# Pooled attention and a max-out MoE on one core: leftover queries of both heads in two column tiles, two pairs in query parts, constant matmuls ahead of the first K

## The chip, the cores and the metric

The kernel runs on one core of a Trainium2 chip. Its time is in device microseconds (us) for one execution of the whole program, the median of several. Beside it stands the profile of one execution, whose span runs from the first instruction to the end of the last.

Engines by their names in the profile: PE is TensorE, the matrix engine (PEld are its weight loads), ACT is ScalarE, DVE is VectorE, POOL is GpSimd, SP is SyncE, which here only issues DMAs. A matmul of TensorE holds one operand as weights in its 128x128 array and streams the other through it. An array can be used whole (128*128 in the profile), as two halves of 64 rows each (64*128), or as two halves of 64 columns each.

## The reference

```python
q, k, v: (8, 8, 1152, 64)             # batch, heads, sequence, head width
q_pool = q.reshape(B, H, S // 2, 2, D).mean(axis=3)          # 576 queries a head
scores = (1 / sqrt(D)) * q_pool @ k^T
attn = exp(scores - max) / sum
x = (attn @ v).transpose(0, 2, 1, 3).reshape(B * 576, 512)   # 4608 tokens of width 512
h1, h2 = x @ w1, x @ w2                                      # 512 -> 1024
out = max(h1, h2) @ w_out                                    # 1024 -> 512, float32
```

Inputs and the output are float32; the kernel multiplies in bfloat16 and sums in float32.

## The kernel before, in words

**Work.** The 64 heads are 32 pairs, two heads of one batch each; a pair's heads share the array as two row halves, 64 rows of head width each. For each pair K and Q are loaded, cast (Q's neighbouring rows are added: that is the pooling), and transposed, by TensorE for the first pairs and by transposing DMAs later. Scores come out transposed, keys on the partitions: per pair nine key tiles of 128 by 576 queries. All pairs' score columns are put end to end and cut into 324 groups of 512 columns (`W`); one group fills a bank for each head, and one ScalarE exp of 128x1024 writes it to `et` in SBUF as bfloat16. `et` has room for two pairs, and the columns of a pair are overwritten by the pair after the next.

**AV.** When a pair's last group is out, `av_jobs` (L471) queues two jobs, one a head. A job is five units, chunks of 128 queries each; a unit is nine matmuls, with 128 columns of `et` as weights and 65 columns of V (64 and a column of ones, which gives the sum of the exps) streaming. 576 queries are four chunks and a half: the fifth covers 64 queries that are wanted and 64 that aren't (columns of the next key tile, or of a pad behind the last). `norm` then takes the reciprocals of the sums and multiplies, on VectorE, into `xnat`, which is transposed into `xT` (by DMA, or by TensorE for the first and the last batch and the last pair of each).

**MoE.** max(h1, h2) @ w_out is computed as relu(x @ (w1 - w2)) @ w_out + x @ (w2 @ w_out). `w21_jobs` makes w2 @ w_out once; `h_jobs` make the relu part for runs of tokens once `xT` holds all four pairs of them; `p_job` makes 128 tokens of the output with twelve matmuls. From some group on (`NARROW`) these run as `Pair`: two jobs share the array as two row halves (L407), in the shape of the scores, so that TensorE needn't change shape between the two.

**Order.** Nothing is scheduled on the chip: while the program is built, `Plan` keeps an estimate of each engine's time, and the loop at L1095 picks TensorE's next unit from what would be ready: a group of scores, an AV unit, MoE units, transposes. `cover` is the estimate of how much exp work ScalarE still has ahead. An AV job once begun goes on whenever anything else or nothing is up (`begun`, L1111); it begins when `cover` is above `START` (1.2 us). All instructions are then emitted in that order, with semaphores where one waits for another.

**Start.** The first pair's K comes in two parts (`K_CUT`, 4 and 5 tiles), cast by ScalarE (`cast_k0`), its queries in two (`Q_CUT`, 256 and 320), added by VectorE. The first pair's score columns are laid out in these two query parts (`strips`, L510), all others in one.

```python
def strips(i):
    for q0, q1 in ((0, Q_CUT), (Q_CUT, SQ)) if i == 0 else ((0, SQ),):
        for t in range(NT):
            yield t, q0, q1
```

The functions that the change touches, with their line numbers:

## Time and profile before

| | |
|---|---|
| median of 3 runs | 372.58 us (371.25 to 373.16) |
| the profiled execution | 372.56 us |
| its span | 370.8 us |
| TensorE, matmuls | 356.4 us busy, 5,918 |
| ScalarE | 315.1 us busy, 305.4 of them exps (336) |
| VectorE | 139.3 us busy |
| GpSimd | 163.1 us busy |
| HBM | 62.91 MB read, 9.44 MB written |

How to read it: a line of a group gives line, engine, operation, output and inputs, their shapes and how often; then the group's busy time in us, the mean of one in ns, the engine's idle time just before them and what ended it. A line in order of time gives its start in us, how long it and those merged with it took together, the engine, and how many. Matmuls overlap on TensorE, so the mean of one (some 190 ns even for a short one) is the time from its start to its end, not the pace at which they follow each other; the pace is read from a stretch of many.

### The profile page before, as it was taken

What the parts mean: (1) busy time and instruction counts of PE and PEld (TensorE: products, weight loads), DVE (VectorE), ACT (ScalarE), POOL (GpSimd) and SP (SyncE); (2) the same over time, 40 slices, a digit from 0 to 9 for tenths busy, and PEclk for the clock granted to TensorE, in tenths of its full rate; (3) what the DMA queues carried; (4) which work ended last, traced back from release to release, by engine and by line L of the source; (5) the groups of instructions that cost most, each with busy time, mean ns of one, the idle gap of its engine ahead of it and who ended that gap; (6) DMA issues with size and microseconds to landing.
All of it is one profiled execution on the core that took longest, in us unless ns stands there. A gap on an engine that the chain in (4) does not pass through costs nothing.

```text
span 370.8 us, 13126 instructions
## 1 busy us (share of the span) xinstructions
PE 356.4 (96%) x5918; PEld 226.2 (61%) x5918; DVE 139.3 (38%) x310; ACT 315.1 (85%) x352; POOL 163.1 (44%) x135
## 2 busy tenths in 40 slices
PE   3799999999899999999999999999999999999996
PEld 2466656656565666666647666766865657665544
DVE  3266864522342244323422332534232424345211
ACT  4999999999899999998898998999999898982211
POOL 2855596464525725482384555545545501000000
PEclk9999999999999999999999999999999999999999
DMA  8999999999999999999999999999999982020145
GB/s 282 408 389 402 359 217 247 220 288 249 344 196 262 282 283 236 280 261 167 359 239 256 269 251 275 299 252 281 331 289 272 272 133 60 2 59 2 23 92 113
DMA packets 91128, 88.10 MB, mean 238 GB/s; under 512 B 63424, under 2 KB 64192, under 8 KB 91072
## 3 DMA queue, kind: packets, MB, share of 16 engines
q1 hardware_dynamic: 90640, 86.87, 92.1%
q8 instruction: 46, 0.75, 0.9%
q10 hardware_dynamic: 432, 0.39, 0.4%
q14 instruction: 10, 0.08, 0.1%
HBM read 62.91 MB, written 9.44 MB: 195 GB/s over the span
## 4 chain that ended last, share of the span: by engine, by line
PE 82%; ACT 12%; DMA 4%; DVE 1%; issue 0%
PE sps L550 18%; PE fb L401 17%; PE fb L407 16%; PE sps L407 15%; PE sps L401 15%; ACT et L557 12%; DMA xT<-xnat 3%; DMA qraw<-in_q_dram 1%; DVE stage L766 0%; PE fb L455 0%; DVE kT L462 0%; DVE qp L378 0%; PE fb L427 0%; PE fb L625 0%; DVE xnat L490 0%
## 5 line engine op out<-in xcount | busy, mean ns | idle before, releaser
L557 ACT ACTIVATE et<-sps 128x1024 bf16<-128x1024 f32 (+1 forms) x336 | 305.4, 1016 | 21.1 <-PE sps L550 19.0
L550 PE MATMUL sps<-qpT,kT 64*128 64x256 bf16 (+7 forms) x1162 | 121.3, 287 | 3.9 <-ACT et L557 2.9
L370 POOL TENSOR_TENSOR qp<-qraw 64x576 bf16<-64x576 f32 x62 | 88.7, 1431 | 62.0 <-DMA qraw<-in_q_dram 38.0
L550 PEld LDWEIGHTS sps<-qpT,kT 64*128 64x128 bf16 x1162 | 47.5, 95 | 53.3 <-ACT et L557 27.7
L384 POOL TENSOR_SCALAR vE<-vraw 128x1152 bf16<-128x1152 f32 x32 | 37.7, 1179 | 57.7 <-DMA vraw<-in_v_dram 36.0
L401 PEld LDWEIGHTS fb<-vE,et 128*128 128x128 bf16 x1755 | 55.7, 97 | 11.1 <-issue 5.7
L401 PE MATMUL fb<-vE,et 128*128 128x65 bf16 x1755 | 61.2, 193 | 0.0
L346 POOL TENSOR_SCALAR kbf<-kraw 128x1152 bf16<-128x1152 f32 x31 | 36.1, 1165 | 29.6 <-DMA kraw<-in_k_dram 26.3
L401 PEld LDWEIGHTS sps<-vE,et 128*128 128x128 bf16 x1125 | 35.7, 97 | 7.3 <-issue 3.3
L401 PE MATMUL sps<-vE,et 128*128 128x65 bf16 x1125 | 39.4, 193 | 0.0
L407 PE MATMUL sps<-xT,wd 64*128 64x512 bf16 (+6 forms) x384 | 36.4, 296 | 0.5 <-DMA xT<-xnat 0.3
L407 PE MATMUL fb<-xT,wd 64*128 64x192 bf16 (+5 forms) x352 | 35.1, 306 | 1.4 <-DMA xT<-xnat 1.4
L407 PE MATMUL fb<-wo,stage 64*128 64x512 bf16 x256 | 36.3, 376 | 0.0
L736 DVE TENSOR_SCALAR stage<-fb 128x512 bf16<-128x512 f32 (+4 forms) x38 | 20.9, 588 | 25.9 <-PE fb L407 24.0
L736 DVE TENSOR_SCALAR stage<-sps 128x512 bf16<-128x512 f32 (+3 forms) x38 | 22.6, 629 | 20.7 <-PE sps L407 17.6
L488 DVE RECIPROCAL rc<-fb 128x5 f32<-128x5 f32 x39 | 7.6, 195 | 58.2 <-PE fb L401 58.2
L407 PE MATMUL sps<-wo,stage 64*128 64x512 bf16 x192 | 27.8, 376 | 0.0
L766 DVE COPY stage<-fb 128x512 f32<-128x512 f32 x16 | 10.3, 687 | 37.3 <-PE fb L407 37.3
L407 PEld LDWEIGHTS fb<-xT,wd 64*128 64x128 bf16 x352 | 16.4, 94 | 9.7 <-DMA xT<-xnat 1.9
L407 PEld LDWEIGHTS sps<-xT,wd 64*128 64x128 bf16 x384 | 16.5, 94 | 9.3 <-DMA xT<-xnat 0.5
L766 DVE COPY stage<-sps 128x512 f32<-128x512 f32 (+1 forms) x16 | 10.2, 671 | 31.2 <-PE sps L401 17.4
L490 DVE TENSOR_TENSOR xnat<-fb,rc 128x320 bf16<-128x320 f32 x39 | 19.2, 491 | 1.3
(65 smaller groups left out, 217.6 us busy)
## 6 DMA issues: line engine op xcount, KB each, us to landing
vraw<-in_v_dram SPq DMA_DIRECT2D x32, 576.0 KB, 6.7
kraw<-in_k_dram SPq DMA_DIRECT2D x31, 576.0 KB, 6.2
qraw<-in_q_dram SPq DMA_DIRECT2D x31, 576.0 KB, 6.0
out_dram<-stage SPq DMA_DIRECT2D x70, 128.0 KB, 4.1
xT<-in_moe_w_dram SPq DMA_DIRECT2D x4, 512.0 KB, 11.8
stage<-in_moe_w_out_dram SPq DMA_DIRECT2D x4, 512.0 KB, 15.2
stage<-in_moe_w_dram SPq DMA_DIRECT2D x4, 512.0 KB, 13.1
kT<-kbf SPq DMA_TRANSPOSE x27, 5.7
```

Source lines behind the costliest of these rows:

```text
L346: op("POOL", lambda g: g.tensor_scalar(kbf[s][:, :, :, :].rearrange("p t h d -> p h t d"), kraw[r][:, :, :, :], 1.0, 1.0, ALU.mult, ALU.mu ...
L370: op("POOL", lambda g, half=half, a=a: g.tensor_tensor(qp[s][:, :, half, :], a[:, :, 0, :], a[:, :, 1, :], ALU.add), r=[f"qraw{r}"], w=[f" ...
L384: op("POOL", lambda g: g.tensor_scalar(vE[r][:, :, :, 0:D].rearrange("p t h d -> p h t d"), vraw[r][:, :, :, :], 1.0, 1.0, ALU.mult, ALU.m ...
L401: last = e.matmul(fb[ms[0]][:, at:at + rhs.shape[-1]], lhs, rhs, start=start, stop=stop)
L407: last = e.matmul(fb[m][:, at:at + rhs.shape[-1]], lhs[rows(half)], rhs[rows(half)], start=first, stop=fin)
L488: dve(lambda e: e.reciprocal(rc[half][:, :], a[:, :, 64:65]), [f"f{m}"], [f"rc{half}"], 0.19)
L490: dve(lambda e: e.tensor_tensor(xnat[xs][:, i % NHP, :, half * D:half * D + D], a[:, :, 0:D], rc[half][:, :].unsqueeze(2).to_broadcast([P, ...
L550: last = e.matmul(sps[r][:, h, col:col + hi - lo], kT[i % 3][rows(h), t, :], qpT[i % 3][rows(h), lo:hi], start=True, stop=True)
L557: op("ACT", lambda e: e.activation(et2[:, :, c:c + z - a], sps[r][:, :, a - g * W:z - g * W], EXP, scale=scale), r=[f"s{r}"], w=keys + [f" ...
L736: dve(lambda e: e.tensor_scalar_max(to, a, 0.0), [f"f{m}"], w, 0.1 + many * size / 960.0)
L766: dve(lambda e: e.tensor_copy(osb[o][:, 0:n], fb[m][:, 0:n]), [f"f{m}"], [f"osb{o}", f"f{m}"], 0.1 + n / 966.0)
```

## The change

1. **Leftover queries.** A job of AV now has units for whole chunks only (four). The leftover 64 queries of both heads are one unit of the second head's job (`ends`): 18 matmuls with 64 weight columns each, the heads alternating. Head 0 writes partitions 0 to 63, head 1 partitions 64 to 127 of the second head's bank: two column tiles. It has a shape of its own in the plan ("c"). `norm` takes the reciprocal of four columns for the first head and five for the second, multiplies four chunks for each, and the leftover of each head in a multiplication of its own on 64 partitions. The pad of 64 columns in `et` goes; the unused half of `xnat`'s last chunk is set to zero once.
2. **Query parts.** Pairs 2 and 3 (`halves`) are laid out as pair 2's first 256 queries, pair 3's first 256, pair 2's other 320, pair 3's other 320. Each part has AV jobs, a normalization and a transpose of its own. What must be read before a place of `et` is overwritten is now kept by the place (`needs_av`, keys of 64 columns) and no longer by the pair.
3. **Start.** A memset of ones and nine matmuls of 128x512 on it (`warm_up`), whose results nothing reads, stand ahead of the first query transposes. The first K comes by DMA in 2 and 7 tiles, is cast in 2, 2 and 5, and transposed in the same cuts. The order of the first loads changes (the first weights come after three more loads).
4. **Choice of the next unit.** The fixed thresholds become rows of digits, one for every 5 us of the plan's time. An AV job once begun may pause (`hold`). Where nothing is up for more than 0.12 us, the plan waits in steps of 0.05 us and chooses again. The plan's estimates for instruction fetch and for transposing DMAs change, which alters no instruction but the order.

```diff
+ORDER = dict(
+    first="k2 v1 q2 k3 k4 q3 w0 q4 v2 w2 v3 w1",
+    halves=(2, 3),
+    k_cuts=(0, 2, 4, 9),
+    q_cut=256,
+    warm=9,
...
+    start="0056465136572767164476550756344413564146064671544542152344732214530673110601",
+    pause="3046380040400300000000800390900003030040704300700009039000040003000064000848",
...
-                self.pages[k] = t + 1.65 + 0.9 * max(0.0, self.dma_free - t)
+                self.pages[k] = t + (5.7 if self.dma_free > t + 0.5 else 3.0)
...
-            seen = self.dma_free + (1.2 if mode == "t" else 0.8)
+            seen = self.dma_free + (2.2 if mode == "t" else 0.8)
...
-        et = sbuf([P, 4 * PW + HP], BF16, "et")
+        et = sbuf([P, 4 * PW], BF16, "et")
...
             def ones(g):
-                g.memset(et[:, 4 * PW:], 0.0)
+                for s in range(2):
+                    g.memset(xnat[s][:, :, NCH, :], 0.0)
...
+        def warm_up():
+            op("DVE", lambda e: e.memset(kbf[1][:, 0, :, :], 1.0), w=["kbf1"], cost=0.1)
+            for n in range(WARM):
+                op("PE", lambda e: e.matmul(
+                    fb[0][:, :].rearrange("p (a x) -> p a x", x=P), kbf[1][:, 0, :, :].rearrange("p h d -> p (h d)"),
+                    kbf[1][:, 0:1, :, :].rearrange("p t h d -> p t (h d)").to_broadcast([P, 4, P]),
+                    start=True, stop=True), r=["kbf1"], w=["f0"], cost=0.427, n=2)
...
+            def ends(e, m):
+                at = (NCH - j0) * 66
+                for t in range(NT):
+                    for half in range(2):
+                        a = half * 2 * PW + spot(i, t, NCH * P)
+                        last = e.matmul(fb[m][rows(half), at:at + 65], et[:, a:a + HP], vE[vs][:, t, half, 0:65],
+                                        start=t == 0, stop=t == NT - 1)
+                return last
+
             def norm(half):
+                jf = min(j1, NCH)
+                both = half and j1 > NCH
...
                 def evac(m):
...
+                    for h in range(2 if both else 0):
+                        dve(lambda e, h=h: e.tensor_tensor(
+                            xnat[xs][0:HP, i % NHP, NCH, h * D:h * D + D], a[rows(h), n, 0:D],
+                            rc[half][rows(h), n:n + 1].to_broadcast([HP, D]), ALU.mult),
...
-            return [Job("a", [mm_unit(reads(half, sb), 0.264, chunk(half, sb)) for sb in range(NCH + 1)],
-                        norm(half), nb=i) for half in range(2)]
+            jobs = []
+            for half in range(2):
+                units = [mm_unit(reads(sb, P), 0.264, chunk(half, sb)) for sb in range(j0, min(j1, NCH))]
+                if half and j1 > NCH:
+                    units.append(Unit(reads(NCH, HP), 0.29, "c", go=ends, many=18))
+                jobs.append(Job("a", units, norm(half), nb=(i, part)))
+            return jobs
...
+        def order():
+            for i in range(NPAIR):
+                if i in HALVES:
+                    if i == HALVES[0]:
+                        for part in range(2):
+                            for p in HALVES:
+                                yield p, part, *spans(p)[part], p if part else HALVES[0]
...
-        load_k(0, 0, K_CUT, "ACT")
-        load_k(0, K_CUT, NT)
+        load_k(0, 0, K_CUTS[1], "ACT")
+        load_k(0, K_CUTS[1], NT)
         load_q0(q_half, QU, "qraw0", "d_q0")
-        cast_k0(0, K_CUT, "kraw0.0")
+        warm_up()
+        for lo, hi in zip(K_CUTS, K_CUTS[1:]):
+            cast_k0(lo, hi, "kraw0" if lo else "kraw0.0")
         cast_q0(0, q_half, "qraw0.0", "a")
-        cast_k0(K_CUT, NT, "kraw0")
...
-            begun = [c for c in avs if len(running[c[3]].job.units) <= NCH]
-            if begun and (rest or not up):
+            begun = [c for c in avs if len(running[c[3]].job.units) < running[c[3]].job.full]
+            level, pause, chain = 0.8 + 0.1 * knob("start"), knob("pause"), knob("chain")
+            hold = pause and begun and (up and cover < 0.1 * pause if plan.mode != "s"
+                                        else cover <= level and (rest or up))
+            if chain < 9 and plan.mode != "s":
+                level = 0.2 * chain
+            if begun and not hold and (rest or not up):
                 emit_unit(running[min(begun)[3]])
...
+                soonest = min(first_up[0], 1e9 if ts is None else ts)
+                if now() + 0.12 < soonest < 1e9:
+                    plan.free["PE"] = now() + 0.05
```

More of the change, by code (lines that the diff above doesn't have):

```diff
@@ L296, in bass_funnel_attn__then__act_maxout2_kernel, with knob @@
         plan = Plan()
+        FIRST, HALVES, Q_CUT = ORDER["first"], ORDER["halves"], ORDER["q_cut"]
+        K_CUTS, WARM, DEPTH = ORDER["k_cuts"], ORDER["warm"], ORDER["depth"]
+        K_PE, Q_PE, X_PE = range(ORDER["k_pe"]), ORDER["q_pe"], ORDER["x_pe"]
+        NAR, CALM, AHEAD, GATE = ORDER["narrow"], ORDER["calm"], ORDER["ahead"], ORDER["gate"]
+        def knob(name):
+            row = ORDER[name]
+            return int(row[min(len(row) - 1, int(now() / ORDER["bin"]))])
         op = plan.op
@@ L469, in ktrans_pe, with av_jobs @@
             return jobs
-        def av_jobs(i):
+        def av_jobs(i, part):
             b, h0 = i // NHP, 2 * (i % NHP)
-            es = i % 2
             vs = i % 3
             xs = b % 2
-            need = [f"et{es}.{g - first(i)}" for g in range(first(i), after(i))] + [f"vE{vs}", "pad"]
+            j0, j1 = (x // P if x < SQ else NCH + 1 for x in spans(i)[part])
             def chunk(half, sb):
@@ new lines, in norm, with xn_of @@
+                return evac
+            jobs = []
[5 more added lines that the diff above has]
+            return jobs
+        def xn_of(i, part=None):
+            return [f"xn{i // NHP % 2}.{2 * (i % NHP) + half}.{p}" for half in range(2)
+                    for p in ((0, 1) if part is None or i not in HALVES else (part,))]
@@ L963, in refill @@
             kinds = [r.job.kind for r in running]
-            for kind in "qkxa" + ("wh" if queue["a"] and "p" in kinds else "wph"):
-                while queue[kind] and spare and bank_at(spare[0]) <= now() + (9.0 if tail else 0.3):
+            for kind in "qkxa" + ("wh" if queue["a"] and "p" in kinds else "whp" if knob("weights") else "wph"):
+                while queue[kind] and spare and bank_at(spare[0]) <= now() + (9.0 if tail else 0.1 * knob("look")):
                     wide = queue[kind][0].two or NARROW <= nxt < NGR and queue[kind][0].split
-                    if wide and (len(spare) < 2 or pairs >= (1 if queue["a"] else 2)):
+                    if wide and (len(spare) < 2 or pairs >= (1 if queue["a"] and knob("lanes") else 2)):
                         break
@@ L1008, in emit_scores @@
             scores(g)
-            for p in pairs_of(g):
-                if g == after(p) - 1:
-                    queue["a"].extend(av_jobs(p))
+            for part in sorted(part for part, last in ends_in.items() if last == g):
+                queue["a"].extend(av_jobs(*part))
             nxt += 1
```

256 lines of the change are left out of this document (144 added, 112 removed).

## The prediction

> **What bounds the kernel now.** I read the busy shares first, then the slices, then the chain of waits, then the busy time by stage and the order of time at both ends.
>
> ```profile
> span 370.8 us, 13126 instructions
> PE 356.4 (96%) x5918; PEld 226.2 (61%) x5918; DVE 139.3 (38%) x310; ACT 315.1 (85%) x352; POOL 163.1 (44%) x135
> ...
> PE   3799999999899999999999999999999999999996
> ...
> ACT  4999999999899999998898998999999898982211
> ...
> PE 82%; ACT 12%; DMA 4%; DVE 1%; issue 0%
> ```
>
> TensorE is busy for 96% of the span and carries 82% of the chain that ended last. ScalarE is at 85%, but its slices fall to 2 and 1 in the last four, where TensorE stays at 9 but for the very end. So there are two stages: exps and everything else side by side until about 332 us, then a tail that TensorE works through alone. The end is set by TensorE's backlog: what doesn't fit beside the exps is paid for in the tail.
>
> By stage (columns: window, its sum, then busy time of PE, PEld, DVE, ACT, POOL):
>
> ```profile
> 10.00:20.00 10.00, 7.87 (x128) 4.99 (x128) 2.48 (x7) 10.00 (x12) 7.60 (x6) 1.00 1.03 405
> 20.00:40.00 20.00, 18.87 (x356) 12.84 (x351) 12.68 (x28) 19.97 (x24) 11.37 (x9) 1.00 1.04 397
> 40.00:80.00 40.00, 40.00 (x626) 23.33 (x625) 20.98 (x38) 38.72 (x44) 25.14 (x18) 1.00 1.09 260
> 80.00:120.00 40.00, 38.58 (x667) 23.98 (x663) 13.74 (x31) 36.10 (x40) 19.94 (x17) 1.00 1.12 258
> ...
> 280.00:320.00 40.00, 39.68 (x749) 26.13 (x745) 14.53 (x36) 37.23 (x43) 11.34 (x9) 1.00 0.73 163
> ...
> 340.00:350.00 10.00, 10.00 (x76) 5.04 (x74) 3.19 (x5) 3.17 (x6) 0.00 (x0) 1.00 0.01 2
> 350.00:360.00 10.00, 10.00 (x48) 4.50 (x47) 1.38 (x2) 0.81 (x3) 0.00 (x0) 1.00 0.44 95
> ```
>
> TensorE idles for 2.1 us in 10 to 20, 1.1 in 20 to 40 and 1.4 in 80 to 120, and hardly otherwise. In the first of these ScalarE is busy for all 10 us: there the exps bound. From 40 us on TensorE is full while ScalarE has 1.3 to 3.9 us to spare per 40. So time taken from TensorE's work after some 40 us comes off the end nearly one for one, whether it is used to fit more MoE matmuls beside the exps or to feed ScalarE sooner.
>
> **The change part by part.**
>
> The span is 370.8 us and this execution's time 372.56 us, so 1.76 us lie around the span; the median of the three runs, 372.58, is the same within 0.02, and I sum against 372.56.
>
> *1. Leftover queries.* Before, every pair's AV is five chunks of nine 128x65 matmuls for each head; the fifth covers 64 real queries and 64 that aren't wanted. That is 18 of 90 matmuls a pair, 576 of 2,880. After, these 576 have 64-column weights, the heads alternating between the lower and the upper half of the array's columns. The rows that price them:
>
> ```profile
> 18.05 1.53 PE L401 MATMUL fb<-vE,et 128*128 128x65 bf16 x45
> ...
> 20.40 0.45 PE L401 MATMUL fb<-vE,et 128*128 128x65 bf16 x9
> ...
> 20.78 0.39 PE L550 MATMUL sps<-qpT,kT 64*128 64x448 bf16 x4
> ...
> 21.11 0.45 PE L401 MATMUL fb<-vE,et 128*128 128x65 bf16 x9
> ```
>
> 45 matmuls end 1.53 us after the first begins. One alone has a mean of 193 ns:
>
> ```profile
> L401 PE MATMUL fb<-vE,et 128*128 128x65 bf16 x1755 | 61.2, 193 | 0.0
> L401 PEld LDWEIGHTS fb<-vE,et 128*128 128x128 bf16 x1755 | 55.7, 97 | 11.1 <-issue 5.7
> L550 PE MATMUL sps<-qpT,kT 64*128 64x448 bf16 x140 | 25.0, 351 | 0.0
> L550 PE MATMUL sps<-qpT,kT 64*128 64x64 bf16 x144 | 14.2, 191 | 0.6 <-ACT et L557 0.6
> ```
>
> (1530 - 193) / 44 = 30 ns from start to start, weight load included, though one load has a mean of 97 ns: the loads are hidden behind other matmuls. Removed: 576 x 30 = 17.3 us. No row shows two column tiles. The nearest that shows two halves of the array at work at once is this one, with row halves:
>
> ```profile
> 337.96 0.20 PE L625 MATMUL sps<-ident,xnat 64*128 64x64 bf16 x1
> 337.96 0.20 PE L625 MATMUL fb<-ident,xnat 64*128 64x64 bf16 x1
> ...
> 338.00 0.19 PE L625 MATMUL sps<-ident,xnat 64*128 64x64 bf16 x1
> ...
> 338.03 0.19 PE L625 MATMUL sps<-ident,xnat 64*128 64x64 bf16 x1
> ...
> 338.09 0.19 PE L625 MATMUL sps<-ident,xnat 64*128 64x64 bf16 x1
> ```
>
> The two halves start in the same hundredth, and the next pair 30 to 40 ns later; from 337.96 to 338.09 are four steps, 33 ns each. The upper bound is no overlap: 576 x 30 = 17.3 us, no saving, and worse if the loads come into the open (a rival below). The lower bound is a pair in the time of one matmul: 288 x 30 = 8.6 us. I take the row pairs' 33 ns, 288 x 33 = 9.5 us, because they are the same kind of case: two small tiles, alternating. Saved: 17.3 - 9.5 = 7.8 us.
>
> The Trainium skill speaks against this: TensorEngine Tiling (Array Packing), section Restrictions and Gotchas, says that column tiling excludes fast weight load. TensorE: Matmul & The Clock Gate, section LDWEIGHTS, then gives one column per 1/1.2 ns, as an estimate 53 ns for 64 columns; with 18 such loads in a row a pair's leftover would be 0.96 us instead of 0.54, and the sum would come to some 387 us. No run so far shows a load of 64 columns.
>
> *2. Changes of tile shape.* In the rows at 20.40 to 21.11, nine AV matmuls need 9 x 30 = 0.27 us, yet the scores behind them start after 0.38: 0.11 for the change from whole array to row halves. Those scores are 448 and 64 columns wide; 448 cost 351 - 191 = 160 ns more than 64 in the mean of one, or 0.4 ns a column, so 512 need about 0.21, and AV starts after 0.33: 0.12 for the way back. In the built programs' instruction order TensorE changes shape 181 times before and 200 times after: the leftover is a shape of its own, but there are fewer whole-array stretches. 19 x 0.11 = +2.1 us. That no change costs extra where it falls into a wait would make it 0; full price is the upper bound. I take +2.1, since TensorE hardly waits.
>
> *3. The start.*
>
> ```profile
> 4.59 0.63 ACT L352 ACTIVATE kbf<-kraw 128x512 bf16<-128x512 f32 x1 [2.01 <-DMA kraw<-in_k_dram]
> ...
> 4.88 0.39 PE L427 MATMUL fb<-ident,qp 64*128 64x64 bf16 x4 [4.88 <-DVE qp L378]
> ...
> 5.28 0.61 PE L455 MATMUL fb<-ident,kbf 128*128 128x128 bf16 x4
> ...
> 5.49 0.74 ACT L352 ACTIVATE kbf<-kraw 128x640 bf16<-128x640 f32 x1 [0.26 <-DMA kraw<-in_k_dram]
> ...
> 6.40 1.03 PE L550 MATMUL sps<-qpT,kT 64*128 64x256 bf16 x8 [0.52 <-DVE kT L462]
> ...
> 7.05 1.94 ACT L557 ACTIVATE et<-sps 128x1024 bf16<-128x1024 f32 x2 [0.83 <-PE sps L550]
> ...
> 8.34 1.15 POOL L346 TENSOR_SCALAR kbf<-kraw 128x1152 bf16<-128x1152 f32 x1 [6.71 <-DMA kraw<-in_k_dram]
> ...
> 9.32 15.69 ACT L557 ACTIVATE et<-sps 128x1024 bf16<-128x1024 f32 x17 [0.33 <-PE sps L550]
> ...
> 10.07 1.14 PE L455 MATMUL fb<-ident,kbf 128*128 128x128 bf16 x9
> ...
> 15.40 0.68 PE L455 MATMUL fb<-ident,kbf 128*128 128x128 bf16 x9
> ```
>
> The same nine K transposes take 1.14 us at 10.07 and 0.68 at 15.40: TensorE starts at half pace, although the granted clock reads 1.00. The nine constant matmuls of 512 columns put work ahead of the first K. At half pace (0.8 ns a column) they take up to 3.7 us and, begun near 1 us, end near 5, when the first query transposes were due anyway (4.88); bounds: those are 0.3 us late, or nothing is. K comes in cuts of 2, 2 and 5 tiles. The two ScalarE casts of before, 0.63 for 4 tiles and 0.74 for 5, give 0.11 a tile and 0.19 fixed, so the last two casts, 0.41 and 0.74, follow the second part of K (landed by 5.49) until about 6.65, and the first exp can start there instead of at 7.05. The third exp, at 9.32 now, would follow two (1.94) at about 8.6; but the second group's scores now stand behind seven K transposes, so I take 8.8. ScalarE bounds this stage, so the whole program shifts: -0.5 us, bounds -1.0 and +0.3.
>
> *4. Pairs 2 and 3 in query parts.* 18 more score pairs (1,198 matmuls for 1,162) over the same columns, nine query transposes, one more normalization each. At 30 ns or less an instruction that is under 1 us, in a stage where TensorE has 1.1 us idle: 0, bounds 0 and +1. Their first 256 queries reach the MoE sooner, but in the instruction order as many MoE columns stand ahead of the 64th score group as before (26,600 before, 25,900 after, half-array ones counted half), so no gain is booked.
>
> *5. Normalization.* Per pair the two heads' reciprocal and multiplication were 195 + 491 ns each. Now four chunks each, and two narrow multiplications:
>
> ```profile
> L490 DVE TENSOR_TENSOR xnat<-fb,rc 128x320 bf16<-128x320 f32 x39 | 19.2, 491 | 1.3
> L488 DVE RECIPROCAL rc<-fb 128x5 f32<-128x5 f32 x39 | 7.6, 195 | 58.2 <-PE fb L401 58.2
> L639 DVE COPY xT<-fb 128x64 bf16<-128x64 bf16 x6 | 1.1, 182 | 0.0
> ```
>
> Four fifths of the streaming plus twice about 182 ns (the nearest 64-wide row) add about 0.2 us a pair, 6 us in all, hidden behind VectorE's 62% idle time. What it delays is the release of the second head's bank, by some 0.3 us; if nothing else were ready, that would cost 32 x 0.3 = 9.6 us. MoE units and the other bank are there to run: 0.
>
> *6. Pauses and time-dependent thresholds* decide only order. In that order the work up to the last score group is 1 us longer for the shape changes and otherwise equal (columns weighed at 0.4 ns), and the work behind it falls from 34.8 to 27.8 us: 7 us less tail, which agrees with 1 to 3. Which waits appear, order doesn't tell.
>
> ```profile
> L407 PE MATMUL fb<-xT,wd 64*128 64x512 bf16 x96 | 13.6, 377 | 1.4 <-DMA xT<-xnat 1.4
> ```
>
> Bounds: the 1.4 us that MoE waited for a transposing DMA goes, with most of the 3.2 us before 40, together -4; or new waits of like size appear, +3. I take 0. The removed memset of a pad and those added on 64-wide rows lie on POOL, idle until 8.34; the reordered first loads cost SP nothing new in number, and the weights still arrive before their first use in the order.
>
> Sum: -7.8 + 2.1 - 0.5 = -6.2, so 372.56 - 6.2 = **366.4 us**.
>
> **The rivals.**
>
> *Loads in the open (slower).* At the leftover of every pair, 64-column weights aren't loaded beside the matmul that runs. If a load is half of the 97 ns of a 128-column one, 48 ns, and the 18 queue up, the leftover takes 0.87 us for 0.54 before: 32 x 0.33 = +10.6; with +2.1 - 0.5 that is 384.8 us. It decides against the change from 27 ns a matmul on: 576 x (30 - 27) = 1.7 covers points 2 and 3. For it: no row shows such loads hidden. Against it: whole-array loads of 97 ns are hidden at a pace of 30, and so are those for row halves. The skill's rule above is this rival.
>
> *No overlap, loads hidden.* The tiles take turns at 30 ns: saving 0, time 372.56 + 2.1 - 0.5 = 374.2, no change to be told. For it: the tiles share all rows, which the row halves don't. Against it: they share no columns and no weights.
>
> *The order gains too.* Shape and overlap as forecast, and the waits fall by the 4 us of point 6: 362.4. For it: there are such waits, 1.4 and 2.1 + 1.1 us. Against it: early idle time is ScalarE's bound, not an order's.
>
> **How the numbers follow.** Forecast 0.66, order gains 0.13, no overlap 0.09, loads in the open 0.12. The forecast's own range: the pair at 30 to 40 ns, the start and half the waits' bounds give 363.5 to 369.5. Leaving out 384.8, and the outer halves of the others, the range is 361 to 372. About 0.5% (1.9 us, near the spread of the three runs) can't be told from no change. Faster: 0.66 + 0.13 + 0.02 = 0.81; same: 0.07; slower: 0.12.
>
> **What would show it.** Right: a leftover group of 18 lasting about 0.3 us plus the last one's 0.19; the last score group near 331, and the tail from there to TensorE's end shorter by 6 to 7 us; the third exp near 8.8; the nine transposes at 10 us in 0.7; VectorE up by 6 us. Wrong: a group of 18 over 0.6 us between starts; the last score group late by more than 3 us; waits of TensorE on VectorE's narrow multiplications; the idle time of TensorE between 40 and 330 grown.

## The result, and the profile after

| kernel | median, us | lowest to highest | runs |
|---|---|---|---|
| before | 372.67 | 371.08 to 376.04 | 20 |
| changed | 369.49 | 365.77 to 374.54 | 20 |

The changed kernel takes 0.9887 of the time of before, with a 95% interval of 0.9861 to 0.9913: 1.1% faster, where the forecast of 366.4 us meant 1.65%. This ratio leaves out executions in a slower state, among them six of the changed kernel's 20 (371.48 us and up); with all of them in, the medians above give 0.9915. The median lies inside the forecast's range.

Two executions of the changed kernel were profiled: one of 373.06 us, in which TensorE's clock was halved twice, and one of 367.81 us. Where not said otherwise, "changed" below is the second; its span is 366.1 us, 4.7 less than the 370.8 of before. First its page: busy time by engine, slices, and the chain that ended last.

```profile
span 366.1 us, 13557 instructions
PE 354.9 (97%) x6093; PEld 226.8 (62%) x6096; DVE 151.5 (41%) x394; ACT 313.8 (86%) x350; POOL 164.3 (45%) x136
...
PE   8789999998999999999999999999999999999996
...
ACT  5999999997999999999999998999979998895311
...
PE 89%; DMA 5%; ACT 2%; POOL 1%; DVE 1%; issue 1%; SPq 0%; POOLq 0%
```

TensorE still ends everything, and at 97% of a shorter span. VectorE has 151.5 us for 139.3 before. The first digit of TensorE's slices, 8 for 3, is the nine constants. By stage, with the columns of before (window, length, then busy time of PE, PEld, DVE, ACT, POOL):

```profile
10.00:20.00 10.00, 8.81 (x135) 5.71 (x136) 3.17 (x9) 9.30 (x12) 9.67 (x8) 1.00 1.04 405
20.00:40.00 20.00, 18.13 (x391) 13.29 (x388) 15.35 (x37) 19.82 (x24) 10.24 (x8) 1.00 1.04 399
40.00:80.00 40.00, 39.52 (x721) 25.93 (x718) 21.95 (x55) 38.72 (x44) 27.35 (x19) 1.00 1.12 281
80.00:120.00 40.00, 38.80 (x670) 24.68 (x668) 14.62 (x39) 36.59 (x41) 21.12 (x17) 1.00 1.10 264
```

From 10 to 40 us ScalarE was busy for 29.12 us, where it was busy for 29.97 before: the start got worse, not better. From 40 to 120 TensorE is idle for 1.7 us, about as before (1.4), but not for the same reason, as will be seen. The end, on TensorE, in order of time: the last score group, and the last matmuls, of the changed kernel and then of before.

```profile
333.35 0.40 PE L654 MATMUL sps<-qpT,kT 64*128 64x512 bf16 x2
...
361.92 1.04 PE L458 MATMUL sps<-wo,stage 128*128 128x256 bf16 x8
```

```profile
330.99 0.38 PE L550 MATMUL sps<-qpT,kT 64*128 64x512 bf16 x2
...
366.69 1.04 PE L401 MATMUL sps<-wo,stage 128*128 128x256 bf16 x8
```

The last score group starts at 333.4 (331.0 before), and TensorE ends at 363.0 (367.7): 29.6 us of tail for 36.7. The tail got 7.1 us shorter, as forecast, and reached its start 2.4 us late. The question is where those 2.4 us, and some more in the median, went.

### The profile page after: what moved, and what is told of

Same layout as the page of the kernel before. It is cut to its first block, busy times and chain, and to the rows that moved or that the text cites. A ratio compares the mean times of both kernels' runs of the same rounds, so it can differ in the third digit from the quotient of the medians.

```text
span 371.3 us, 13557 instructions
## 1 busy us (share of the span) xinstructions
PE 357.2 (96%) x6093; PEld 228.3 (61%) x6096; DVE 151.0 (41%) x394; ACT 314.2 (85%) x350; POOL 164.9 (44%) x136
## 4 chain that ended last, share of the span: by engine, by line
PE 89%; ACT 5%; DMA 2%; issue 1%; POOL 1%; SPq 1%; DVE 0%; POOLq 0%
PE fb L464 20%; PE sps L654 20%; PE sps L464 19%; PE sps L458 13%; PE fb L458 13%; ACT et L661 5%; PE fb L549 3%; DMA vraw<-in_v_dram 2%; PE sps L549 1%; PE sps L730 0%; DVE stage L840 0%; POOL qp L427 0%; POOL vE L441 0%; PE fb L512 0%; POOL kbf L403 0%
## 5 line engine op out<-in xcount | busy, mean ns | idle before, releaser
L654 PEld LDWEIGHTS sps<-qpT,kT 64*128 64x128 bf16 x1198 | 49.8, 95 | 47.5 <-ACT et L661 21.8
L464 PE MATMUL sps<-xT,wd 64*128 64x256 bf16 (+5 forms) x424 | 62.4, 295 | 1.2 <-issue 1.2
L464 PE MATMUL fb<-xT,wd 64*128 64x256 bf16 (+6 forms) x408 | 60.5, 297 | 2.7 <-issue 2.5
L464 PE MATMUL fb<-wo,stage 64*128 64x512 bf16 x272 | 59.0, 376 | 0.0
L464 PE MATMUL sps<-wo,stage 64*128 64x512 bf16 x208 | 49.4, 376 | 0.0
L458 PEld LDWEIGHTS fb<-vE,et 128*128 128x128 bf16 x1296 | 42.8, 98 | 10.0 <-issue 5.6
L840 DVE TENSOR_SCALAR stage<-sps 128x512 bf16<-128x512 f32 (+4 forms) x43 | 25.4, 607 | 37.5 <-PE sps L464 34.5
L464 PEld LDWEIGHTS sps<-xT,wd 64*128 64x128 bf16 x424 | 30.0, 94 | 10.4 <-issue 1.5
L464 PE MATMUL fb<-w,xT 64*128 64x512 bf16 x136 | 30.4, 377 | 0.0
L840 DVE TENSOR_SCALAR stage<-fb 128x512 bf16<-128x512 f32 (+3 forms) x36 | 21.5, 610 | 13.5 <-PE fb L464 12.5
L464 PE MATMUL sps<-w,xT 64*128 64x512 bf16 x104 | 26.5, 377 | 0.0
```

The source lines that it names most:

```text
L458: last = e.matmul(fb[ms[0]][:, at:at + rhs.shape[-1]], lhs, rhs, start=start, stop=stop)
L464: last = e.matmul(fb[m][:, at:at + rhs.shape[-1]], lhs[rows(half)], rhs[rows(half)], start=first, stop=fin)
L654: last = e.matmul(sps[r][:, h, col:col + hi - lo], kT[i % 3][rows(h), t, :], qpT[i % 3][rows(h), lo:hi], start=True, stop=True)
L840: dve(lambda e: e.tensor_scalar_max(to, a, 0.0), [f"f{m}"], w, 0.1 + many * size / 960.0)
```

## The experiments

Each run was timed against the kernel before on the same chip; ratios are to it, with a 95% interval. Rows that the changed kernel and an experiment have in common bear different line numbers where the experiment's edit moved them.

**The changed kernel again** gave the profile above.

> The changed kernel unchanged, for a second profile. In the first profile TensorE loses 2.5, 1.5 and 1.2 us at three places to the arrival of its own instructions, and its clock is halved from 10.75 to 20.99 us and from 273.6 to 277.0. Theory A (what is missing from the forecast is lost to late instructions and the clock, which vary from run to run): these places or their lengths differ here, and the time differs with them. Rival (a fixed cost of the new order, the same in each run): the same losses at the same places. Time 366 to 371 us.

370.56 us in 6 runs, ratio 0.9899 [0.9849, 0.9949]. The gain is there, and the spread is too: one kernel, 367.81 to 371.76.

**Are the two column tiles at work at once?** The one edit makes the tiles take turns: all nine multiplications of one head, then all nine of the other.

```diff
-                for t in range(NT):
-                    for half in range(2):
+                for half in range(2):
+                    for t in range(NT):
```

> The leftover's 18 matmuls in the same 64-column shape, but head 0's nine first and then head 1's nine, so that neighbours use the same half of the columns; order otherwise kept. If the two column tiles work side by side, and the gain is theirs: a group takes 18 x 30 = 0.54 us instead of 0.31, 32 x 0.23 = +7.4 us, some 376. If a load of 64 columns is exposed when neighbours share a tile: 0.87 us a group, +18 us. Rival (the pace of the leftover doesn't count because other work bounds): within 2 us of the changed kernel.

374.47 us in 12 runs, ratio 1.0029 [0.9989, 1.0069]: the whole gain is gone. The same leftover in the two orders of time, changed kernel first (start, length from the first start to the last end, count):

```profile
58.48 1.27 PE L458 MATMUL fb<-vE,et 128*128 128x65 bf16 x36
59.68 0.47 PE L549 MATMUL fb<-vE,et 128*64 128x65 bf16 x18
60.09 0.61 PE L654 MATMUL sps<-qpT,kT 64*128 64x64 bf16 x8
```

```profile
59.70 1.27 PE L458 MATMUL fb<-vE,et 128*128 128x65 bf16 x36
60.89 0.66 PE L549 MATMUL fb<-vE,et 128*64 128x65 bf16 x18
61.48 0.61 PE L654 MATMUL sps<-qpT,kT 64*128 64x64 bf16 x8
```

One such matmul has a duration of 0.195 us, so from these rows the 18 starts lie within 0.47 - 0.195 = 0.275 us when the heads alternate, and within 0.465 when they take turns. The starts in the traces give 0.28 for 31 of the 32 pairs (0.51 for one) and 0.46 for all 32: 33 ns for two, or 27 ns for each. The tiles do work at once. 32 pairs times 0.18 make 5.8 us. How much of it reaches the median is less sure: the two profiled executions differ by 5.8 (373.61 and 367.81), but 0.9 of that was lost before the fortieth exp had ended (45.47 and 44.54), and on that chip the medians differ by 3.9 us and the ratios by 0.013, or 4.8 us. The loads, in the groups by line and form (busy time, mean ns):

```profile
L549 PEld LDWEIGHTS fb<-vE,et 128*64 128x64 bf16 x468 | 9.5, 111 | 1.8 <-issue 0.4
L549 PE MATMUL fb<-vE,et 128*64 128x65 bf16 x468 | 12.5, 197 | 0.0
```

A load of 64 columns takes 111 ns, more than one of 128 columns took for the whole array (97). It isn't sped up, as the section Restrictions and Gotchas of TensorEngine Tiling (Array Packing) in the Trainium skill has it; but at 16 to 27 ns from start to start it is hidden all the same, so the rule doesn't set the time.

**Does the start matter, and the constants?** Two kernels: one with the nine constants at 16 columns in place of 512, and one which has that and also moves the transposes of the second pair's first keys behind the next score group.

```diff
-                    fb[0][:, :].rearrange("p (a x) -> p a x", x=P), kbf[1][:, 0, :, :].rearrange("p h d -> p (h d)"),
-                    kbf[1][:, 0:1, :, :].rearrange("p t h d -> p t (h d)").to_broadcast([P, 4, P]),
+                    fb[0][:, 0:16], kbf[1][:, 0, :, :].rearrange("p h d -> p (h d)"),
+                    kbf[1][:, 0, 0, 0:16],
```

> The nine constant matmuls stream 16 columns instead of 512; the order of all instructions is kept. If the warm-up gains what was forecast (third exp earlier by 0.5 us): slower than the changed kernel by 0.5 us or a little more. Rival: TensorE's clock falls back to half at 10.75 us because too little follows, and the warm-up only moves the slow stretch to a worse place: then the clock opens near 13 us as before the change, and the time falls by 1 to 2 us.

> The constant matmuls with 16 columns, and the first half of the second pair's K transposes, with its copy, behind the score group that follows it instead of ahead. If the start lost time because TensorE stood at these transposes (until GpSimd's cast, 9.8 us) with scores ready behind them: the gap of ScalarE at 10.6 to 11.1 us closes and the 20th exp ends at 25.2 to 25.5 us, after 25.9 with the small warm-up, 26.5 and 27.7 with the full one; time 0.5 to 1 us below the small warm-up's, some 369.8. Rival (loads bound this stage, not the order): the 20th exp ends at 25.9 again.

370.58 us in 10 runs (0.9922 [0.9891, 0.9953]) and 369.32 in 6 (0.9896 [0.9855, 0.9936]): neither can be told from the changed kernel. Had the constants gained what was forecast, the first would have taken 0.5 us more, and its rival expected 1 to 2 us less; neither shows, and 0.5 us is less than these intervals can tell. ScalarE's order of time shows what happens. Changed:

```profile
6.81 1.02 ACT L661 ACTIVATE et<-sps 128x1024 bf16<-128x1024 f32 x1 [0.30 <-PE sps L654]
8.21 2.86 ACT L661 ACTIVATE et<-sps 128x1024 bf16<-128x1024 f32 x3 [0.38 <-PE sps L654]
11.77 18.64 ACT L661 ACTIVATE et<-sps 128x1024 bf16<-128x1024 f32 x21 [0.70 <-PE sps L654]
```

With the transposes moved:

```profile
7.89 11.74 ACT L661 ACTIVATE et<-sps 128x1024 bf16<-128x1024 f32 x12 [0.38 <-PE sps L654]
20.26 1.02 ACT L661 ACTIVATE et<-sps 128x1024 bf16<-128x1024 f32 x1 [0.62 <-PE sps L654]
21.90 1.02 ACT L661 ACTIVATE et<-sps 128x1024 bf16<-128x1024 f32 x1 [0.62 <-PE sps L654]
23.56 6.72 ACT L661 ACTIVATE et<-sps 128x1024 bf16<-128x1024 f32 x8 [0.63 <-PE sps L654]
```

Before, the third exp started at 9.32 and 17 ran without a gap, 0.92 us apart, so the fifth started at 11.1. Changed, the first exp is 0.24 us earlier (6.81 for 7.05), but the fifth starts at 11.77. TensorE's rows say why (in brackets: the idle time before, and what ended it):

```profile
7.56 1.69 PE L654 MATMUL sps<-qpT,kT 64*128 64x256 bf16 x12
10.10 0.45 PE L484 MATMUL fb<-ident,qp 64*128 64x64 bf16 x5 [0.85 <-DVE qp L435]
10.48 0.71 PE L512 MATMUL fb<-ident,kbf 128*128 128x128 bf16 x5
11.12 1.04 PE L654 MATMUL sps<-qpT,kT 64*128 64x256 bf16 x10
```

From 9.25 on TensorE stands before the transposes of the first pair's last 320 queries, with the second pair's key transposes and the scores that ScalarE needs queued behind them. VectorE is the one that is late, in its own order of time:

```profile
7.13 0.29 DVE L519 COPY kT<-fb 128x256 bf16<-128x256 bf16 x1 [1.03 <-PE fb L512]
7.67 0.49 DVE L519 COPY kT<-fb 128x640 bf16<-128x640 bf16 x1 [0.24 <-PE fb L512]
8.19 1.85 DVE L435 TENSOR_TENSOR qp<-qraw 64x320 bf16<-64x320 f32 x2
```

```profile
5.92 0.42 DVE L462 COPY kT<-fb 128x512 bf16<-128x512 bf16 x1 [0.32 <-PE fb L455]
6.38 0.98 DVE L378 TENSOR_TENSOR qp<-qraw 64x320 bf16<-64x320 f32 x2
8.12 0.49 DVE L462 COPY kT<-fb 128x640 bf16<-128x640 bf16 x1 [0.76 <-PE fb L455]
```

These are the changed kernel's rows and then those of before: K in three cuts means three copies to `kT`, and the sum of the last 320 queries (`qp<-qraw`) now stands behind the third of them, at 8.19 and not at 6.38. There it ran into GpSimd's cast of the second pair's keys:

```profile
8.55 1.15 POOL L403 TENSOR_SCALAR kbf<-kraw 128x1152 bf16<-128x1152 f32 x1 [6.07 <-DMA kraw<-in_k_dram]
```

The second of the sum's two instructions began at 8.68, behind the start of the cast, and took 1.36 us, where it takes 0.49 in the profile of before. With 0.49 the sum would have ended at 9.17, about when TensorE came to the transposes (9.25). So the stop of 0.85 us in this execution is this meeting, and the third copy counts here by pushing the sum into it. In the other profiled execution of the changed kernel the sum stood at 7.39, took 0.98 and held TensorE up by 0.40 us, and the next wait was on the cast itself:

```profile
9.81 0.45 PE L512 MATMUL fb<-ident,kbf 128*128 128x128 bf16 x5 [1.06 <-POOL kbf L403]
10.19 0.61 PE L654 MATMUL sps<-qpT,kT 64*128 64x256 bf16 x10
```

With the second pair's transposes moved, the exps from the second to the thirteenth run without a gap from 7.89 on. But the twentieth ended at 28.24, where 25.2 to 25.5 was expected: in that execution TensorE's clock, as its opening stands in the trace, came up only at 21.8 us, and at half pace ScalarE had to wait for scores three times, 0.62 us each. The clock opened at 13.0 us in the profile of before and at 13.8 in the changed kernel's. In the changed kernel's other execution it opened at 3.9, while the constants ran, and closed again at 10.75; the granted clock (the third number from the end) there:

```profile
8.00:10.00 2.00, 0.53 (x11) 0.40 (x10) 0.69 (x2) 2.00 (x3) 1.16 (x1) 1.00 1.00 387
10.00:12.00 2.00, 2.00 (x27) 1.03 (x24) 0.92 (x2) 1.42 (x3) 1.89 (x2) 0.69 1.04 408
...
14.00:18.00 4.00, 3.83 (x36) 1.87 (x31) 1.03 (x3) 4.00 (x5) 3.92 (x5) 0.50 1.05 400
...
20.00:22.00 2.00, 2.00 (x47) 1.65 (x45) 0.61 (x2) 1.53 (x2) 1.05 (x2) 0.75 1.02 407
```

Full-width constants had it open near 4 us in two of four profiled executions (one of them of the kernel without pauses, below), and both times it closed again 6.8 us later, behind a stretch in which TensorE mostly stood (0.53 us of matmuls in 8 to 10). These spells, 6.83 us open and 10.24 at half, are multiples of 3.41 us, the window that the section Part 1: The HAM clock gate of TensorE: Matmul & The Clock Gate in the Trainium skill states.

**What is the order worth?** Three kernels have an order made anew, from other work or with another threshold: before with the column tiles and their normalization alone; changed without pauses; before with AV begun from 1.3 us of cover in place of 1.2.

```diff
-    pause="3046380040400300000000800390900003030040704300700009039000040003000064000848",
+    pause="0",
...
-        START = 1.2
+        START = 1.3
```

> The kernel before with the column tiles alone (leftover unit, its normalization, the memset), its own start, thresholds and pairs in one part. By the forecast's terms: -7.8 us for the tiles, and 210 changes of shape for 181 in its order, +3.2: 368.0 us. If the tiles are all of the gain it is at or below the changed kernel; if pauses, parts and the start carry part of it: 370 or more.

> The row of pauses set to zero: AV jobs never pause. In the order so made TensorE changes shape 224 times instead of 200, and 4.6 us of streaming move from before the last score group to behind it. By the terms: +24 x 0.1 = +2.4 us, 373. If pausing carries little: within 1 us of the changed kernel. If the order as a whole is tuned to its thresholds, whatever the terms say: 376 or more.

> The kernel before with one threshold, START, at 1.3 instead of 1.2; nothing else. In its order there are 180 changes of shape instead of 181, but 39.8 us of streaming stand behind the last score group instead of 35.1, as in the kernel before with tiles only (39.2). If a longer tail in the order costs its length, as that run suggests: 376 to 378. If only the sum of streaming and changes counts: 372.5 as before.

| kernel | median, us (runs) | ratio | shape changes in order | TensorE waits for exps in the profile |
|---|---|---|---|---|
| before, tiles alone | 382.56 (6) | 1.0227 [1.0161, 1.0292] | 210 | 7.2 us, 14 times |
| changed, no pauses | 379.73 (4) | 1.019 [1.0137, 1.0242] | 224 | 2.9, 7 |
| before, 1.3 us | 379.66 (4) | 1.0173 [1.0122, 1.0223] | 180 | 4.0, 10 |
| before | 372.67 (20) | 1 | 181 | 2.9, 7 |
| changed | 369.49 (20) | 0.9887 [0.9861, 0.9913] | 200 | 1.6, 4 |

The waits are those of score matmuls for the exp that empties their bank, from the list of waits of each. Each of these three is 7 to 10 us slower than the kernel that it was made from, the first in spite of the tiles, which by the forecast's terms should have brought it to 368.0. In the profiles about half of this lies in the tail: from the last score group to TensorE's end the first takes 40.9 us and the third 41.3, where before takes 36.7; without pauses the last score group comes 5.2 us later than in the changed kernel's profile and the tail is 4.8 us longer (34.4 for 29.6). So what the tiles save can't be seen at all where the order is made anew with the old thresholds; and the pauses, which I priced at 0, are worth 9 to 10 us with the other thresholds left as they are. Whether pairs 2 and 3 in query parts gain or lose by themselves wasn't tried.

**Stalls that wait for nothing.** The first profile of the changed kernel has gaps in the midst of groups of equal matmuls, with no wait that the profile shows ("issue"). TensorE's loads there:

```profile
271.32 0.09 PEld L464 LDWEIGHTS fb<-xT,wd 64*128 64x128 bf16 x1
273.89 0.77 PEld L464 LDWEIGHTS fb<-xT,wd 64*128 64x128 bf16 x7 [2.48 <-issue]
```

and the queue that carries instructions, in the DMA view of three stretches on end, 264.5 to 271.3, 271.3 to 272.0 and 272.0 to 273.9: only the middle one has a line for it.

```profile
q8 instruction: 1, 0.02, 8.4%
```

Over the whole span that queue moved 46 packets before and 48 after (page, DMA queues), 0.75 and 0.79 MB: 16 KB each. That makes the some 12,000 TensorE instructions come in pages of about 256. The packet here began at 271.45, and TensorE, whose last load had ended at 271.41, went on at 273.89, 2.44 us later. In the changed kernel's second profile the same place stalls again, for less, and so does another one that the first profile has too (1.47 us at 85.89):

```profile
85.14 0.09 PEld L464 LDWEIGHTS sps<-xT,wd 64*128 64x128 bf16 x1 [1.48 <-issue]
...
269.93 0.44 PEld L464 LDWEIGHTS fb<-xT,wd 64*128 64x128 bf16 x7 [0.54 <-issue]
```

Counting every TensorE instruction of the trace from the start (matmuls, loads, and the few that only wait), these two are number 2753 and 9410 in both executions. So of the two theories of the first run here each is half right: the places stay, the lengths don't. Over all profiles there are 24 such gaps of more than 0.5 us after 30 us, and each stands at a count that leaves 193 or 194 when divided by 256, whatever work is there; two of them are in the kernel before with the 1.3 us. Sums by execution (gaps over 0.5 us after 40 us): before 0; changed 5.1 and 2.0; with small constants 6.4; heads in turn 1.8; with transposes moved 2.9.

If the late page is the cause, pushing TensorE's program by half a page moves the ends of pages to other work, and pushing it by a whole page brings them back. Four kernels: the 9 constants of 512 columns replaced by 72 of 64 (63 matmuls and as many loads more, 126 instructions, in the same time), twice; by 137 of 16 (128 and 128, a page); and before with 63 of 16 columns ahead.

```diff
+            def short(e):
+                for x in range(8):
+                    last = e.matmul(fb[0][:, x * 64:x * 64 + 64], kbf[1][:, 0, :, :].rearrange("p h d -> p (h d)"),
+                                    kbf[1][:, 0, 0, :], start=True, stop=True)
+                return last
...
-                op("PE", lambda e: e.matmul(
...
+                op("PE", short, r=["kbf1"], w=["f0"], cost=0.427, n=2)
```

> The nine constant matmuls of 512 columns become 72 of 64 columns: the same streaming time, 63 more matmuls, so 126 more instructions (with their loads) ahead of everything else; order otherwise kept. In all profiles of the changed kernel TensorE stalls at the same counted instruction, 2753 and 9410 (of matmuls and loads), for 0.5 to 2.6 us, and the instruction queue's DMA begins some 2.5 us before. Theory A (instructions come in pages of 256, and the next page is late): stalls are at counted instructions 2753 + 256 n again, that is in other work than before, and the sum of such stalls changes, to 0 to 6 us; the time changes with it by up to 3 us either way. Rival (the stalls belong to the work at those places): they stay with the same work, at counts near 2879 and 9536, and the time is as the changed kernel's, 370.5.

> The same kernel as in the run that moved the instruction pages by 126 (72 constants of 64 columns), again, as the mark for the two runs beside it. Page theory: no TensorE stall of more than 0.6 us without a wait after 40 us, a span near 363.5, a median of 366 to 368. Rival, that the 3.7 us it gained over the changed kernel were the chip of that batch: a median near 370.

> The changed kernel with 137 constants of 16 columns ahead in place of its 9 constants: 128 more multiplications, with their loads 256 more instructions of TensorE, which is one whole page. Page theory: every piece of later work stands at the same place in its page as in the changed kernel, so stalls of 0.5 to 2.6 us come back at some of the same work, now at the counted instructions 256 later (3009, 9666 and their neighbours), 2 to 5 us in all, and the median is 369.5 to 371. Rival, that any longer row of constants helps, or a later start: stalls stay away as in the run with 126 more, median 366 to 368.

> The kernel before, with its own order, and 63 constants of 16 columns ahead of it (126 more instructions of TensorE, half a page). Page theory: the kernel before has no stall of more than 0.42 us without a wait after 40 us at its own place; moved by half a page it may get some: 372 to 376, never below 372 by more than its interval. Rival, that constants ahead bring the gain by themselves (an open clock): 369 to 371.

| kernel | median, us (runs) | ratio | gaps over 0.5 us after 40 us, at count |
|---|---|---|---|
| half a page | 366.84 (6) | 0.9838 [0.98, 0.9875] | none (one of 0.9 us at 32.4) |
| half a page, again | 367.07 (6) | 0.9849 [0.981, 0.9888] | 8386, 8641: 1.7 us |
| a whole page | 368.7 (6) | 0.9882 [0.985, 0.9914] | 3009, 4546, 9666: 3.5 us |
| before, half a page | 373.38 (12) | 0.9998 [0.9969, 1.0027] | none |

The last three ran on one chip. With a whole page more the same work stalls again, at the counts named ahead, 2753 + 256 and 9410 + 256. TensorE's loads there:

```profile
84.67 0.09 PEld L467 LDWEIGHTS sps<-xT,wd 64*128 64x128 bf16 x1 [1.18 <-issue]
...
271.37 0.43 PEld L467 LDWEIGHTS fb<-xT,wd 64*128 64x128 bf16 x7 [1.74 <-issue]
```

At half a page these places are gone (the eight loads of that row run through at 268.33), and what stalls are left stand at other work. So the cause of these gaps is shown: the page of instructions comes late. Why it comes late in one execution and not in another is open. Two expectations missed: the second run at half a page was to have no stall over 0.6 us and has one of 1.2, and the whole page was to take 369.5 us at least and took 368.7. Constants ahead do nothing for before by themselves. The size is less sure than the cause: 1.6 us in the medians between the two on one chip, whose intervals overlap, and 2.0 us between the mean ratio of the two half-page runs (0.9844) and that of four runs at the old place (changed twice, small constants, whole page: 0.9898). The start doesn't explain it: the fortieth exp ends at 44.16 and 45.45 in the half-page profiles and at 44.37 with a whole page. Whether a page is late is different in each execution, so moving the pages is no cure in general.

**All together.** Half a page, the transposes moved, and multiplications by the unit matrix in the gaps of the first 14 us, so that the clock stays open.

```diff
+            if u.filler and len(fills) > filled[0]:
+                filled[0] += 1
+                op("PE", fill, r=["ident"], w=fk(ms), cost=0.0, mode=plan.mode)
```

> The changed kernel with 22 constants of 208 columns, with 50 multiplications of the unit matrix in the gaps of the first transposes, so that TensorE does not stand before its clock opens, with the first transposes of the second pair's keys behind the next score group, and in all about as many instructions more as the page shift of 126. If the start is priced as I read it (pages 3.7 us, gap of 0.4 to 0.8 us behind the third exponential, clock opened at 4 and kept): the twentieth exponential ends near 25.2 where it ended at 26.07, and the median is 365 to 366. Rival, that the start is bounded by the casts and the loads and the filling only stands in the way: twentieth exponential at 26 or later, median 367 to 369.

366.51 us in 6 runs, ratio 0.9834 [0.9798, 0.987]: the same as half a page alone. The first exps run without the long gap, and yet the twentieth ends at 25.95, against 25.84 and 26.07 with half a page alone:

```profile
6.70 3.85 ACT L679 ACTIVATE et<-sps 128x1024 bf16<-128x1024 f32 x4 [0.22 <-PE sps L672]
10.78 10.19 ACT L679 ACTIVATE et<-sps 128x1024 bf16<-128x1024 f32 x11 [0.23 <-PE sps L672]
21.26 9.47 ACT L679 ACTIVATE et<-sps 128x1024 bf16<-128x1024 f32 x11 [0.29 <-PE sps L672]
```

That is nearly the rival's figure (26 or later; the theory had 25.2), though the median lies between the two expectations. TensorE again waited 0.8 us for VectorE's sum of the last 320 queries, whose second half began at 8.21, behind the start of GpSimd's cast (8.02), and took 1.34 us for 0.49. No kernel here moved the sum ahead of the third copy; that wasn't tried. The profiled execution also has the longest gap of all, in the middle of one group of 18 leftover loads:

```profile
180.16 0.26 PEld L567 LDWEIGHTS fb<-vE,et 128*64 128x64 bf16 x11
183.26 0.20 PEld L567 LDWEIGHTS fb<-vE,et 128*64 128x64 bf16 x7 [2.84 <-issue]
```

After it the clock was at half from 183.7 to 187.1. The half-page kernel and this one have the lowest medians of all, 1.6 to 4.1 us below those of the changed order at its own place; between the two there is nothing to tell.

## Why the prediction was right, and where its size was off

The direction, the term that carries it and the tail were right; the sum was 3.1 us too low against the median, and 2.1 against 0.9887 of the median before. By its own steps, against the changed kernel's profile (span 4.7 us shorter):

| step | forecast, us | measured, us |
|---|---|---|
| 1 leftover tiles | -7.8 | -7.4 |
| 2 shape changes | +2.1 | +1.9 |
| 3 start | -0.5 | +1.0 |
| 4 query parts | 0 | not separated |
| 5 normalization | 0 | 0 |
| 6 waits for `xT` | 0 (to -4) | -1.7 |
| late pages of instructions | not in the sum | +2.0 |
| sum | -6.2 | -4.2, of -4.7 |

*1.* The row pairs' 33 ns were the right neighbour: two column tiles take 33 ns a pair. The 18 matmuls of a pair hold TensorE for 0.28 + 0.03 = 0.31 us, where 18 at 30 ns took 0.54: 32 x 0.23 = 7.4. "Loads in the open" fell with the hidden 111 ns loads; "no overlap" fell with the heads in turn. That run took 374.47 us, where I had worked out 374.2 for no overlap; the agreement is partly luck, since the start and the late pages, which that sum didn't have, are in it too.

*2.* In the rows of the leftover above, the scores follow 0.41 us after the first of the 18 starts, which take 0.28: 0.41 - 0.28 - 0.03 = 0.1 us for the change. 19 x 0.1 = 1.9.

*3.* Here the step failed. "ScalarE bounds this stage, so the whole program shifts" held, but I took the third exp's lead (8.8 forecast, 9.1 measured, 9.32 before) for that of all that follow. I had looked at the seven key transposes ahead of the second group, and not at the transposes ahead of the groups after it: they wait for VectorE's sum, which the third cut of K pushed back by 1 to 1.8 us (in the profile read here into GpSimd's cast, beside which it took another 0.87), and for that cast itself, and the scores queue behind. The fortieth exp ends at 44.54, for 43.54 before; in the nine profiles with the changed order it ends 0.2 to 2.3 us later than before. The sign "third exp near 8.8" was also the wrong one to watch; the fifth would have told it. And the nine transposes near 10 us did not run in 0.7 us altogether: 0.71 for five and 0.61 for four, at half pace, since the constants did not keep the clock open.

*5.* VectorE rose by 12 us, not 6. The groups by form:

```profile
L563 DVE TENSOR_TENSOR xnat<-fb,rc 128x256 bf16<-128x256 f32 x34 | 14.4, 425 | 1.2
L568 DVE TENSOR_TENSOR xnat<-fb,rc 64x64 bf16<-64x64 f32 x52 | 11.2, 215 | 0.4
```

64 narrow multiplications at 0.215 make 13.8 us, and the 64 wide ones of before (0.491) became 60 of 0.425 and 8 of 0.29, 3.6 less: +10 us. I had counted "about 0.2 us a pair"; it is 0.3. It is hidden, as argued: TensorE's one stall of over 0.15 us behind these lines is 0.41 us, at 33.3.

*6.* The waits of MoE for a transposing DMA (1.4 and 0.3 us) are gone from the list of waits. That is a gain within the bounds, and it hides most of what the pages cost in this profile: TensorE's idle time between 40 and 330 us, a sign of being wrong if it grew, is 2.6 us for 2.4. But "decide only order" was the wrong reason for a price of 0: an order made anew cost 7 to 10 us in three experiments, in two of them with the work unchanged, and that is as much as the tiles bring or more. That it came out near 0 here is most likely because the thresholds had been fitted to this very kernel, which no run tests; as far as the stated reason goes, it was luck.

*The missing term.* The sum had no row for instructions that come late, since the profile of before has no such gap. 2 us in the read profile, 5.1 in the other; by the medians of the page runs about 2. With it and the start's 1.5 us, the forecast's 366.4 becomes 369.9; less the 1.7 of the DMA waits it is 368.2, within 1.3 of the median.

## What to carry to other kernels

When two small operands share the rows of the array and differ in columns, alternating them from one instruction to the next is what makes the overlap: here 33 ns for two, and 27 for each when they take turns. When an order is written out ahead of time, price a change to the work only with the order made again and tuned; otherwise its noise (here up to 10 us) is larger than the term. At the start, follow the lead through the first five or six dependent steps, since a sum queued behind one more copy, two engines away, can give it all back. What another engine does at the same time counts too: here half of that sum, beside a cast, took almost three times as long.

## What the hardware showed beside that

TensorE's own instructions are traffic on a busy machine. A kernel of 12,000 of them fetches 16 KB, for the most part every 5 to 10 us; at the five gaps of the changed kernel's two profiles the fetch started 3.2 to 5.2 us after the page before was entered, and the first instruction of the new page ran 2.4 to 2.6 us after the fetch's start. The section Instruction fetch mechanics of Runtime: NRT & Kernel Launch in the Trainium skill gives the same pages, 16 KiB or 256 instructions, and calls their cost mostly hidden; before agrees (no gap), and the kernels with the changed order don't, with 0.5 to 2.8 us at up to four places. A gap of 2.48 us in the first changed profile was followed by half the clock for 3.4 us, and so was the one of 2.84 with all together, so a gap can cost more than itself; one of 2.53 in the profile with small constants was not. And the page shows a granted clock of 1.00 until the clock's first opening, while the matmuls there go at half pace: nine key transposes took 0.71 and 0.61 us for five and four in the stretch before 13.8 us. VectorE and GpSimd can hold each other up: in the two of the fourteen profiles where the second instruction of the query sum began behind the start of GpSimd's cast (by 0.13 and 0.20 us), it took 1.36 and 1.34 us for 0.49 and ended 0.33 us after the cast; in three where it began ahead of the cast and overlapped it, the cast took 1.21, 1.31 and 1.38 us for 1.15.
